# Spreading 1 / sum with full-size constants, and the last 64 keys of v in a zero-padded tile

## The chip, the cores and the metric

The kernel runs on one core of a Trainium2 chip. The metric is the device time of one execution in microseconds (us). One execution of each kernel was also recorded by the hardware profiler; the engines in it are PE (TensorE matmul), PEld (TensorE weight load), DVE (VectorE), ACT (ScalarE), POOL (GpSimd) and SP (SyncE, which issues most DMAs).

## The reference

Four batches, eight heads of size 64, 576 positions. Per head, scores = q k^T / 8; in each row the 32 largest scores are kept, exponentiated, divided by their sum and multiplied by v. The heads, side by side, make x (576 x 512 per batch), which goes through a gated value projection and a phase mixer:

```python
scores = np.where(scores >= kth, scores, -1e9); scores -= scores.max(-1)
attn = np.exp(scores); attn = attn / (attn.sum(-1) + 1e-9); x = attn @ v
x = (sigmoid(causal_conv5(x)) * (x @ w_val)) @ w_out
theta = x @ w_theta; u = x + w_tok_r @ (x * cos(theta)) + w_tok_i @ (x * sin(theta))
out = u + relu(u @ w_ch)
```

## The kernel before

The attention runs over tiles of 128 query rows. A unit u is a pair of heads (j = 0, 1) of one batch; its 576 query rows are handled in two parts, x = 0 (rows 0 to 255) and x = 1 (rows 256 to 575). There are 16 units, so 32 parts. For each tile PE computes the scores from split q and k (L536, L537), ACT moves them out of PSUM (L550), DVE searches the largest ones (L572 to L599, with help of ACT L585 and POOL L593), ACT takes the exponential (L193), DVE masks and sums (L652), and PE transposes the result: four full 128 x 128 transposes (L665) that ACT copies into pT (L684), and one of the last 64 keys (L669), which uses free columns of a scores bank; ACT copies it into slot 8 of pT (L673). In slot 8 the last 64 keys of head j = 0 lie in partitions 0 to 63, those of j = 1 in partitions 64 to 127.

When a part has all its tiles, `close` ends it:

- the product px with v (L758) has ten matmuls: five chunks c of keys times two heads j. Head j's result goes to PSUM partitions 64j to 64j + 63. Chunks 0 to 3 have 128 keys each, chunk 4 has 64, whose v lies in partitions 64j to 64j + 63 of the fifth slot of the tile v2;
- 1 / sum (tile rs, one column for each query tile and head: 4 columns for x = 0, 5 for x = 1) is transposed on PE (L714) and copied by ACT into rT (L717, 4 or 5 partitions by 128 columns);
- `columns(m)`, for m = 0 and 1, spreads a row of rT over the 64 partitions of its head: one matmul for each j at L731, whose stationary operand is a column of the identity matrix, repeated 64 times. For x = 1 and m = 1 there is also a fifth row, the 64 last queries of both heads, spread by a matmul for each j at L734. These matmuls use free columns of a scores bank: m = 0 stands behind L669 in the first bank, m = 1 behind the scores of the second. ACT copies the bank's part into rb (L738);
- DVE multiplies px by rb (L776).

```python
nc.tensor.matmul(spare[r, :P], row(2 * j + m), rT[:n], start=True, stop=True,
                 skip_group_check=True)
```

Each fp32 matmul is two records of PE in the trace; a transpose is one, and so is a matmul of the split (fp32r) operands. DVE and ACT follow the order in which the program is written. PE, POOL and SP are put in order by a scheduler when the program is built, each instruction as soon as it is due. Between the attention steps PE is given pieces of the projections and of the mixer (L507, L805, L1107, L1126). v of a unit is loaded by three DMAs of SP into the one buffer v2 (L223, and L227 twice); they wait until the px before has read it. The constants are made by POOL at the program's start (L162 to L176).

Of the kernel before, what the change touches and what calls it, by code (L numbers as in the profile page):

```python
# [11 lines left out]
F32 = mybir.dt.float32  # L12
# [78 lines left out]
def mixer(ctx, tc, qT, kT, vt, w_val, conv_t, w_out, w_theta, w_tok, w_ch, out, flag):  # L91
    nc = tc.nc
    safe = flag is None
    P = 128
# [4 lines left out]
    NF = S // P  # L99
    REM = S - NF * P  # L100
# [14 lines left out]
    cp = ctx.enter_context(tc.tile_pool(name="cp", bufs=1))  # L115
    io = ctx.enter_context(tc.tile_pool(name="io", bufs=1))
    sp = ctx.enter_context(tc.tile_pool(name="sp", bufs=1))
    wk = ctx.enter_context(tc.tile_pool(name="wk", bufs=1))
# [44 lines left out]
    ident = cp.tile([P, P], F32, name="ident")  # L163
# [8 lines left out]
    nc.gpsimd.memset(trig_bias[64:], 0.0)  # L172
    half_pi = cp.tile([P, 1], F32, name="half_pi")
    nc.gpsimd.memset(half_pi, math.pi / 2)
    magic = cp.tile([P, 1], F32, name="magic")
    nc.gpsimd.memset(magic, MAGIC)  # L176

# [40 lines left out]
    def load_v(part):  # L218
        u = part["u"]
        b, hp = divmod(u, NP)  # L220
        v2 = io.tile([P, NF + 1, P], F32, tag="v2", name=f"v2_{u}_{part['x']}")
        vu = vt[b, :, hp * P : (hp + 1) * P]
        nc.sync.dma_start(v2[:, :NF, :], vu[: NF * P].rearrange("(c p) d -> p c d", p=P))  # L223

        for j in range(2):
            r = slice(REM * j, REM * j + REM)
            nc.sync.dma_start(v2[r, NF, 64 * j : 64 * j + 64], vu[NF * P :, 64 * j : 64 * j + 64])  # L227
        part["v"] = v2
        if u // NP not in SPLIT:
            parts[u, 1]["v"] = v2  # L230
# [457 lines left out]
    def diagonal(hp):  # L688

        if not diagonals:  # L690
            all_of = ml.tile([P, 2 * NC * ROOM[1]], F32, tag="room1", name="diagonals")
            diagonals["all"] = all_of[:, : NP * KW * P].rearrange("p (u k w) -> p u k w", u=NP, k=KW)
        if hp not in diagonals:
            diagonals[hp] = diagonals["all"][:, hp]
            nc.gpsimd.tensor_tensor(diagonals[hp], ident.unsqueeze(1).broadcast_to([P, KW, P]),
                                    W["conv"][:, hp, :].unsqueeze(2).broadcast_to([P, KW, P]), ALU.mult)
        return diagonals[hp]

    def close(part):

        u, x = part["u"], part["x"]
        b, hp = divmod(u, NP)
        lo, hi = COLS[x]
        w = hi - lo
        n = 4 + x
        rs = wk.tile([P, 5], F32, tag="rs", name=f"rs_{u}_{x}", bufs=2)
        rT = wk.tile([5, P], F32, tag="rT", name=f"rT_{u}_{x}")
        rb = wk.tile([P, S - CUT], F32, tag="rb", name=f"rb_{u}_{x}")
        nc.gpsimd.tensor_scalar(rs[:, :n], part["sums"][:, :n], 1e-9, None, ALU.add)
        nc.vector.reciprocal(rs[:, :n], rs[:, :n])  # L710
        done = set()

        def rows(spare):
            nc.tensor.transpose(spare[:n, :P], rs[:, :n], ident)  # L714

            def f():
                nc.scalar.copy(rT[:n], spare[:n, :P])  # L717
                done.add("rows")
            return f

        def row(k):
            return ident[:n, k : k + 1].broadcast_to([n, 64])

        def columns(m):


            def on_pe(spare):
                c = P + REM * (m * x)
                for j in range(2):
                    r = slice(64 * j, 64 * j + 64)  # L730
                    nc.tensor.matmul(spare[r, :P], row(2 * j + m), rT[:n], start=True, stop=True,  # L731
                                     skip_group_check=True)
                    if c > P:
                        nc.tensor.matmul(spare[r, P:c], row(4), rT[:n, r], start=True, stop=True,  # L734
                                         skip_group_check=True)

                def f():
                    nc.scalar.copy(rb[:, m * P : m * P + c], spare[:, :c])  # L738
                    done.add(m)
                return f  # L740
            return on_pe

        extras.append((P, rows))
        yield
        yield
        asked = "rows" in done
        if asked:
            extras.extend((P + REM * (x * m), columns(m)) for m in range(2))
        yield
        if x == 0:  # L750
            drain(("val", (u - 5) // NP))
        v, pT = part["v"], part["pT"]
        owed[0] -= 8.3 * w
        px = ps_m.tile([P, w], F32, tag="m", name=f"px_{u}_{x}")
        for c in range(NF + 1):
            for j in range(2):
                r, k = (slice(0, P), j * NF + c) if c < NF else (slice(REM * j, REM * j + REM), 2 * NF)
                nc.tensor.matmul(px[64 * j : 64 * j + 64, :], v[r, c, 64 * j : 64 * j + 64], pT[r, k, :],  # L758
                                 start=(c == 0), stop=(c == NF), skip_group_check=True)
        if x == 0:  # L760
            xt = sp.tile([P, PAD + S], F32, tag="xT", name=f"xT_{u}", bufs=5)
            nc.gpsimd.memset(xt[:, :PAD], 0.0)
            xT.setdefault(b, []).append(xt)
        xt = xT[b][hp]
        yield
        while "rows" not in done:
            yield
            yield
        if not asked:
            extras.extend((P + REM * (x * m), columns(m)) for m in range(2))  # L770
        yield
        yield
        while 1 not in done:
            yield
            yield
        nc.vector.tensor_tensor(xt[:, PAD + lo : PAD + hi], px, rb[:, :w], ALU.mult)  # L776
        there.add((u, x))
        split = b in SPLIT
        if not split and x == 0:
            return  # L780
        if split and x:
            g = gate[b][hp]
        else:
            drain(("gate", (u - GB) // NP))
            g = sp.tile([P, S], F32, tag="gp", name=f"gp_{u}", bufs=GB)
            gate.setdefault(b, []).append(g)
        if not split:
            lo = 0
        g = g[:, lo:hi]
        cw = W["conv"]  # L790
        if hp == NP - 1:
            jobs.append(front(b, (x,) if split else (0, 1)))
            if x:
                jobs.append(back(b))
        yield
        yield
        while lacking["conv"]:
            yield
            yield
        taps = [xt[:, k + lo : k + hi] for k in range(KW)]  # L800
        if split:
            owed[0] -= 1.675 * KW * (hi - lo)
            ps = ps_m.tile([P, hi - lo], F32, tag="m", name=f"pconv_{u}_{x}")
            for k in range(KW):
                nc.tensor.matmul(ps, diagonal(hp)[:, k, :], taps[k], start=(k == 0), stop=(k == KW - 1))  # L805
            yield
            yield
            tabled(g, ps, AF.Tanh, scale=0.5)
            ready.add((u, x))
            return  # L810
        nc.scalar.activation(g, taps[0], AF.Copy, scale=cw[:, hp, 0:1])
        for k in CT:
            ct = wk.tile([P, S], F32, tag="ct", name=f"ct_{u}_{x}_{k}")[:, : g.shape[1]]
            nc.scalar.activation(ct, taps[k], AF.Copy, scale=cw[:, hp, k : k + 1])
            nc.gpsimd.tensor_tensor(g, g, ct, ALU.add)
            yield
            yield
        if not CT:
            yield
            yield  # L820
        rest = [k for k in range(1, KW) if k not in CT]
        for k in rest:
            nc.vector.scalar_tensor_tensor(g, taps[k], cw[:, hp, k : k + 1], g, ALU.mult, ALU.add)
            if k == rest[1] and len(rest) > 2 or k == rest[-1]:
                yield
                yield
        tabled(g, g, AF.Tanh, scale=0.5)
        ready.add((u, x))
# [355 lines left out]
    for b in range(B):  # L1184
        late = b == B - 1
        f = 1.275 if b in THREE else 1.675
# [19 lines left out]
    def drain(key):  # L1206

        n = 0
        while key[1] >= 0 and key not in done:
            n += 1  # L1210
            assert n < 1000, (key, [(j.gi_frame.f_code.co_name, j.gi_frame.f_lineno, j.gi_frame.f_locals.get('b')) for j in jobs], sorted(map(str, done))[-40:], len(later), len(mid))
            run_mid()
            now, later[:] = list(later), []
            run(now)
            work(DRAIN)
# [24 lines left out]
    for k, part in enumerate(order):  # L1240
        i0 = part["tiles"][0].i
        u, x = part["u"], part["x"]
# [5 lines left out]
        elif split or x == 0:  # L1248
            when = (i0 - 7, i0 - 5, i0 - 5, i0 - 4, i0 - 3) if split or i0 and order[k - 1]["x"] and order[k - 1]["u"] // NP in SPLIT else (i0 - 9, i0 - 8, i0 - 7, i0 - 6, i0 - 3)
            a = (u, x if split else None)  # L1250
            for step, do in zip(when, (load_heads, split_high, split_low, *(
                    lambda u, x, j=j: double(u, j, x) for j in range(2)))):
# [144 lines left out]
```

## Time and profile before

| | us |
|---|---|
| median of 3 runs (lowest, highest) | 849.69 (846.92, 850.99) |
| the profiled execution's own time | 849.38 |
| its span, first to last instruction | 847.3 |
| PE busy | 754.7 (89%) |
| DVE busy | 679.4 (80%) |
| ACT busy | 640.3 (76%) |
| POOL busy | 438.5 (52%) |

The profile is of one execution. Matmuls are pipelined, so the length of a record tells little; how far apart the starts of two records lie tells what PE needs between them. The chain of work that ended last goes back from the last instruction, at each step to what released it or to the instruction before it on its engine: what stands on it set the time.

### The profile page before, as it was taken

How to read it: one execution, taken by the hardware profiler on the slowest of the kernel's cores; microseconds unless marked ns; L12 is line 12 of the kernel's file. 1: busy time of each engine (PE TensorE's matmuls, PEld its weight loads, DVE VectorE, ACT ScalarE, POOL GpSimd, SP SyncE). 2: the span in 40 equal slices, each digit the busy share in tenths (PEclk: the TensorE clock that was granted, in tenths of full speed). 3: DMA queues.
4: the chain of work that ended last, by engine and by line, in shares of the span. 5: the costliest groups of instructions: out<-in, count | busy, mean ns of one | idle time of the engine just before them, and what ended most of it. 6: DMA issues, size and time to landing. Idle time of an engine off the chain costs nothing.

```text
span 847.3 us, 16018 instructions
## 1 busy us (share of the span) xinstructions
PE 754.7 (89%) x4606; PEld 577.5 (68%) x4606; DVE 679.4 (80%) x2786; ACT 640.3 (76%) x1573; POOL 438.5 (52%) x575
## 2 busy tenths in 40 slices
PE   4478999969898899899699989999999899999995
PEld 3345667535655666677587666768897666798895
DVE  6999999879977888899889879989998686353521
ACT  6688898889778777889689887789987784336511
POOL 4876665545544545457667725537796143004600
PEclk9997799979999899999899999999999999999998
DMA  6566665634440243337455543234664300061002
GB/s 171 140 167 189 163 171 161 176 90 127 117 107 15 58 144 82 94 77 240 112 171 168 151 136 83 44 83 100 184 176 122 100 1 15 1 211 45 2 1 61
DMA packets 73602, 94.37 MB, mean 111 GB/s; under 512 B 13728, under 2 KB 37152, under 8 KB 73504
## 3 DMA queue, kind: packets, MB, share of 16 engines
q1 hardware_dynamic: 73184, 92.82, 40.3%
q8 instruction: 39, 0.64, 0.3%
q14 instruction: 59, 0.48, 0.2%
q10 hardware_dynamic: 320, 0.43, 0.2%
HBM read 49.96 MB, written 13.11 MB: 74 GB/s over the span
## 4 chain that ended last, share of the span: by engine, by line
PE 48%; DVE 27%; ACT 11%; POOL 6%; issue 4%; DMA 3%; SPq 1%; ACTq 0%; POOLq 0%
PE py L1107 8%; PE px L758 7%; DVE cand L572 6%; PE pval L507 5%; DVE thrs L599 4%; PE px2t L507 4%; PE pth L507 4%; PE ph L507 3%; PE pt L665 3%; DVE s L652 3%; PE py L1126 3%; PE ps L536 3%; POOL y L593 2%; DVE cand L578 2%; PE ps L537 2%
## 5 line engine op out<-in xcount | busy, mean ns | idle before, releaser
L593 POOL TENSOR_TENSOR y<-s,n 128x576 f32<-128x576 f32 x144 | 190.6, 1324 | 164.8 <-DVE thrs L599 118.6
L572 DVE MAX8 cand<-s 128x8 f32<-128x96 f32 x864 | 210.2, 244 | 1.4 <-ACT s L550 1.4
L652 DVE SCALAR_TENSOR_TENSOR s<-s,thrs,e 128x576 f32<-128x576 f32 x144 | 139.4, 968 | 9.7 <-ACT e L193 9.7
L585 ACT ACTIVATE n<-s,tops 128x576 bf16<-128x576 f32 x144 | 112.0, 778 | 39.6 <-POOL y L593 18.7
L550 ACT ACTIVATE s<-ps 128x256 f32<-128x256 f32 (+1 forms) x288 | 103.7, 406 | 32.9 <-PE ps L731 15.8
L665 PE MATMUL pt<-ident,s 128*128 128x128 f32 x576 | 96.2, 288 | 26.7 <-ACT pT L684 12.6
L1107 PE MATMUL py<-w_tok,z 128*128 128x256 f32 (+1 forms) x432 | 116.8, 410 | 3.4 <-DVE z L966 3.4
L599 DVE MAX8 thrs<-y 128x8 f32<-128x584 f32 x144 | 109.3, 759 | 6.8 <-POOL y L594 6.4
L758 PE MATMUL px<-pT,v 128*64 128x256 f32 (+3 forms) x640 | 106.7, 432 | 9.0 <-ACT pT L684 8.8
L193 ACT ACTIVATE e<-s,least 128x576 f32<-128x576 f32 x144 | 110.7, 769 | 0.5 <-DVE s L652 0.4
L665 PEld LDWEIGHTS pt<-ident,s 128*128 128x128 f32 x576 | 68.8, 145 | 55.6 <-ACT pT L684 22.4
L536 PE MATMUL ps<-kh_None,q 128*128 128x256 f32 x240 | 92.0, 390 | 4.1 <-ACT s L550 2.2
L684 ACT COPY pT<-pt 128x512 f32<-128x512 f32 x128 | 73.1, 571 | 28.5 <-PE pt L665 15.4
L1107 PEld LDWEIGHTS py<-w_tok,z 128*128 128x128 f32 x432 | 77.8, 191 | 24.0 <-DVE z L966 5.0
L758 PEld LDWEIGHTS px<-pT,v 128*64 128x64 f32 (+1 forms) x640 | 43.6, 140 | 57.6 <-issue 26.5
L576 DVE MAX8 tops<-cand 128x8 f32<-128x48 f32 x432 | 82.7, 191 | 0.1
L537 PE MATMUL ps<-kl_None,q 128*128 128x256 f32 x240 | 71.4, 300 | 0.0
L536 PEld LDWEIGHTS ps<-kh_None,q 128*128 128x128 f32 x240 | 46.4, 193 | 21.1 <-ACT s L550 6.1
L536 PE MATMUL ps<-kh,q 128*128 128x256 f32 (+1 forms) x80 | 37.5, 475 | 20.3 <-ACT s L550 8.6
L578 DVE MATCH_REPLACE8 cand<-tops,cand 128x48 f32<-128x48 f32 x288 | 55.1, 191 | 0.0
L673 ACT COPY pT<-ps 64x128 f32<-64x128 f32 (+1 forms) x160 | 39.3, 245 | 12.6 <-PE ps L669 5.8
L537 PEld LDWEIGHTS ps<-kl_None,q 128*128 128x128 f32 x240 | 47.0, 196 | 2.5 <-issue 0.9
(209 smaller groups left out, 1693.4 us busy)
## 6 DMA issues: line engine op xcount, KB each, us to landing
kh_None<-kh_None SPq DMA_DIRECT2D x48, 144.0 KB, 2.6
kl_None<-kl_None SPq DMA_DIRECT2D x48, 144.0 KB, 2.7
v<-in_vt_dram SPq DMA_DIRECT2D x20, 256.0 KB, 3.5
out_dram<-x2T SPq DMA_DIRECT2D x16, 256.0 KB, 3.2
w<-ch SPq DMA_DIRECT2D x16, 256.0 KB, 4.3
w<-theta SPq DMA_DIRECT2D x16, 256.0 KB, 5.4
raw_hi<-in_w_tok_dram SPq DMA_DIRECT2D x14, 256.0 KB, 4.1
kh<-kh SPq DMA_DIRECT2D x24, 144.0 KB, 2.6
```

The source lines that it names most:

```text
L193: ins = nc.scalar.activation(out, src, func, **more).ins
L507: nc.tensor.matmul(ps[o : o + n], x, y, start=(i + k == 0), stop=(i == last and k == len(ways) - 1), skip_group_check=(n < P))
L536: nc.tensor.matmul(bank[:, :w], q2, kh[:, lo:hi], start=(j == js[0]), stop=False)
L537: nc.tensor.matmul(bank[:, :w], q2, kl[:, lo:hi], start=False, stop=(j == js[-1]))
L572: nc.vector.max(d["cand"][:, k, 8 * x : 8 * x + 8], s_tiles[i][:, x * SUB : (x + 1) * SUB])
L585: nc.scalar.activation(n, s_tiles[i], AF.Sign, bias=d["tops"][:, k, KC - 1 : KC], scale=-(1.0 + 2.0 ** -22), accum_out=acc)
L593: nc.gpsimd.tensor_tensor(y[:, :S], s_tiles[i], d.pop(("n", k)), ALU.mult)
L599: nc.vector.max(thrs[:, N - 1 - i : N - 1 - i + NK], d.pop(("y", k)))
L652: nc.vector.scalar_tensor_tensor(p, p, thr(i), e.exp, ALU.is_ge, ALU.mult, accum_out=part["sums"][:, e.slot : e.slot + 1])
L665: nc.tensor.transpose(e.pt[:, c, :], p[:, c * P : (c + 1) * P], ident)
L758: nc.tensor.matmul(px[64 * j : 64 * j + 64, :], v[r, c, 64 * j : 64 * j + 64], pT[r, k, :], start=(c == 0), stop=(c == NF), skip_group_che ...
L1107: nc.tensor.matmul(ps, z[:, m * P : (m + 1) * P], W["tok"][:, w, lo:hi], start=(i + k == 0), stop=(i == NF))
```

## The change

Three constants are added. `spread` (128 x 7 x 64) holds, in the order 0, 2, 1, 3, none, 4, none, the selectors of rows of rT: a slot for row k has ones in partition k and zeros elsewhere, a slot "none" is zero. Two neighbouring slots make a stationary operand of 128 x 128. `rT` becomes one tile of 128 partitions whose rows from 5 on stay zero. `v_last` (128 x 128) takes the last 64 keys of both heads, each head's 64 columns with zeros in the other head's partitions.

At `columns(m)` one matmul takes the place of the two at L731: slots (0, 2) or (1, 3) spread the rows of both heads over all 128 partitions. For the fifth row there are still two matmuls of 64 columns, now with slots (4, none) and (none, 4), which add up in PSUM. At px the fifth chunk multiplies all 128 partitions of slot 8 of pT by v_last.

```diff
+    spread = cp.tile([P, 7, 64], F32, name="spread")
+    nc.gpsimd.memset(spread, 0.0)
+    for i, k in enumerate((0, 2, 1, 3, None, 4)):
+        if k is not None:
+            nc.gpsimd.tensor_copy(spread[:, i, :], ident[:, k : k + 1].broadcast_to([P, 64]))
+    rT = cp.tile([P, P], F32, name="rT")
+    nc.gpsimd.memset(rT, 0.0)
+    v_last = cp.tile([P, P], F32, name="v_last")
+    nc.gpsimd.memset(v_last, 0.0)
...
-        v2 = io.tile([P, NF + 1, P], F32, tag="v2", name=f"v2_{u}_{part['x']}")
+        v2 = io.tile([P, NF, P], F32, tag="v2", name=f"v2_{u}_{part['x']}")
...
-            nc.sync.dma_start(v2[r, NF, 64 * j : 64 * j + 64], vu[NF * P :, 64 * j : 64 * j + 64])
+            nc.sync.dma_start(v_last[r, 64 * j : 64 * j + 64], vu[NF * P :, 64 * j : 64 * j + 64])
...
-        rT = wk.tile([5, P], F32, tag="rT", name=f"rT_{u}_{x}")
...
-        def row(k):
-            return ident[:n, k : k + 1].broadcast_to([n, 64])
+        def rows_of(i):
+            return spread[:, i : i + 2, :].rearrange("p a w -> p (a w)")
...
-                for j in range(2):
-                    r = slice(64 * j, 64 * j + 64)
-                    nc.tensor.matmul(spare[r, :P], row(2 * j + m), rT[:n], start=True, stop=True,
-                                     skip_group_check=True)
-                    if c > P:
-                        nc.tensor.matmul(spare[r, P:c], row(4), rT[:n, r], start=True, stop=True,
-                                         skip_group_check=True)
+                nc.tensor.matmul(spare[:, :P], rows_of(2 * m), rT, start=True, stop=True,
+                                 skip_group_check=True)
+                for j in range(2 if c > P else 0):
+                    nc.tensor.matmul(spare[:, P:c], rows_of(5 - j), rT[:, 64 * j : 64 * j + 64],
+                                     start=(j == 0), stop=(j == 1), skip_group_check=True)
...
-                r, k = (slice(0, P), j * NF + c) if c < NF else (slice(REM * j, REM * j + REM), 2 * NF)
-                nc.tensor.matmul(px[64 * j : 64 * j + 64, :], v[r, c, 64 * j : 64 * j + 64], pT[r, k, :],
+                d = slice(64 * j, 64 * j + 64)
+                of_v, k = (v[:, c, d], j * NF + c) if c < NF else (v_last[:, d], 2 * NF)
+                nc.tensor.matmul(px[d, :], of_v, pT[:, k, :],
                                  start=(c == 0), stop=(c == NF), skip_group_check=True)
```

On PE the first block of a closing part of x = 1 stood so before (ps is a scores bank; a row gives the tiles, and the partitions by columns that are written):

```order
L669 MATMUL ps_0_1869<-ident,s_1270 64x128
L731 MATMUL ps_0_1869<-rT_1_1695,ident 64x128 x2
L536 MATMUL ps_256_1875<-kh_3_1_1737,q_87 128x320
L537 MATMUL ps_256_1875<-kl_3_1_1738,q_87 128x320
L731 MATMUL ps_256_1875<-rT_1_1695,ident 64x128
L734 MATMUL ps_256_1875<-rT_1_1695,ident 64x64
L665 MATMUL pt_1917<-ident,s_1325 128x128 x4
```

and stands so now:

```order
L678 MATMUL ps_0_1867<-ident,s_1274 64x128
L737 MATMUL ps_0_1867<-rT,spread 128x128
L545 MATMUL ps_256_1872<-kh_3_1_1735,q_87 128x320
L546 MATMUL ps_256_1872<-kl_3_1_1736,q_87 128x320
L737 MATMUL ps_256_1872<-rT,spread 128x128
L740 MATMUL ps_256_1872<-rT,spread 128x64 x2
L674 MATMUL pt_1913<-ident,s_1327 128x128 x4
```

The place is the same; two matmuls of 64 partitions became one of 128 (before, the pair L731, L734 stood twice in the second bank, once for each j).

On SP the load of v for unit 3 of batch 0 stood so before:

```order
L227 DMA v_2_0_1214<-in_vt_dram 64x64
L216 DMA kl_1_1218<-in_kT_dram 128x576
L216 DMA ql_1_1220<-in_qT_dram 128x320
L309 DMA raw_hi_120<-in_w_theta_dram 128x512
L309 DMA raw_hi_121<-in_w_theta_dram 128x512
L309 DMA raw_lo_122<-in_w_theta_dram 128x512
L223 DMA v_3_0_1463<-in_vt_dram 128x4x128
```

and stands so now:

```order
L236 DMA v_last<-in_vt_dram 64x64
L225 DMA kl_1_1222<-in_kT_dram 128x576
L232 DMA v_3_0_1464<-in_vt_dram 128x4x128
L225 DMA ql_1_1224<-in_qT_dram 128x320
L318 DMA raw_hi_131<-in_w_theta_dram 128x512
L318 DMA raw_hi_132<-in_w_theta_dram 128x512
L318 DMA raw_lo_133<-in_w_theta_dram 128x512
```

The load of the first four chunks moved ahead of the load of q and of three loads of weights.

On POOL, at the start, the new constants stand between the making of the identity and the last small ones:

```order
L174 MEMSET half_pi 128x1
L176 MEMSET spread 128x448
masks.py:199 AFFINE_SELECT ident<-ident 128x128
L181 MEMSET rT 128x128
L179 COPY spread<-ident 128x64 x5
L183 MEMSET v_last 128x128
L185 MEMSET magic 128x1
```

Before, none of the rows on spread, rT and v_last was there, and the identity was made last.

## Rows read from the trace of the kernel before

**Rows 1.** Stretches: us, busy us (instructions) of PE, PEld, DVE, ACT, POOL; clock, DMA.

```profile
0.00:510.00 510.00, 433.41 (x2457) 311.14 (x2458) 452.19 (x1957) 424.22 (x1068) 294.82 (x411) 0.95 0.50 134
510.00:650.00 140.00, 138.15 (x948) 110.24 (x948) 131.25 (x569) 118.21 (x298) 93.79 (x116) 1.00 0.45 120
650.00:740.00 90.00, 86.33 (x522) 63.92 (x521) 54.40 (x187) 58.09 (x131) 24.35 (x32) 1.00 0.09 28
```

**Rows 2.** The same view of L758 (px) alone, PE and PEld.

```profile
0.00:510.00 510.00, 71.48 (x400) 28.36 (x400) 0.95 0.50 134
510.00:740.00 230.00, 35.24 (x240) 15.23 (x240) 1.00 0.31 84
```

**Rows 3.** Chain that ended last, shares by line: of 0:510, then of 510:740.

```profile
by line: DVE cand L572 7.8%; issue 6.1%; DVE thrs L599 5.9%; PE px L758 5.8%; DVE s L652 4.1%; PE pval L507 3.9%; POOL y L593 3.4%; PE ps L536 3.1%; ACT n L585 3.1%; PE pconv L805 3.0%; DVE cand L578 3.0%; ACT e L193 2.8%; PE pth L507 2.8%;
...
by line: PE py L1107 23.8%; PE px L758 13.5%; PE pt L665 7.4%; PE pth L507 4.8%; PE ph L507 4.1%; PE ps L536 3.8%; PE px2t L507 3.7%; DVE cand L572 3.5%; PE ps L731 3.4%; PE ps L537 3.1%; DVE s L652 2.9%; DVE gp L823 2.7%; DVE thrs L599 2.7
```

**Rows 4.** Timeline of PE, full-size work alone: start us, length, instruction.

```profile
527.49 0.27 PE L669 MATMUL ps<-ident,s 128*64 128x128 f32 x1
...
527.75 0.32 PE L537 MATMUL ps<-kl_None,q 128*128 128x320 f32 x1
527.90 0.60 PE L665 MATMUL pt<-ident,s 128*128 128x128 f32 x4
528.34 0.38 PE L1107 MATMUL py<-w_tok,z 128*128 128x256 f32 x1
```

**Rows 5.** Timeline of PE around the blocks of a part x = 1.

```profile
138.46 0.27 PE L669 MATMUL ps<-ident,s 128*64 128x128 f32 x1
138.67 0.43 PE L731 MATMUL ps<-rT,ident 5*64 5x128 f32 x4
...
139.28 0.30 PE L537 MATMUL ps<-kl,q 128*128 128x320 f32 x1
...
140.00 0.66 PE L665 MATMUL pt<-ident,s 128*128 128x128 f32 x4
140.49 0.81 PE L507 MATMUL px2t<-gp,w_out 128*128 128x256 f32 x3
```

**Rows 6.** Timeline of PE around the second block of a part x = 0.

```profile
341.88 0.30 PE L537 MATMUL ps<-kl_None,q 128*128 128x320 f32 x1
...
342.48 0.55 PE L665 MATMUL pt<-ident,s 128*128 128x128 f32 x3
```

**Rows 7.** Timeline of PE at the end of a px, looked at moment by moment.

```profile
244.11 0.60 PE L758 MATMUL px<-pT,v 128*64 128x256 f32 x4
...
244.32 0.60 PE L758 MATMUL px<-pT,v 128*64 128x256 f32 x4
...
244.85 0.43 PE L758 MATMUL px<-pT,v 64*64 64x256 f32 x2
...
245.12 0.38 PE L758 MATMUL px<-pT,v 64*64 64x256 f32 x2
```

**Rows 8.** Timeline of PE where both blocks of a part stand together.

```profile
692.08 0.27 PE L669 MATMUL ps<-ident,s 128*64 128x128 f32 x1
...
692.86 0.28 PE L714 MATMUL ps<-ident,rs 128*5 128x128 f32 x1
```

**Rows 9.** Timeline of PEld, in the stretch of rows 4.

```profile
527.75 0.51 PEld L665 LDWEIGHTS pt<-ident,s 128*128 128x128 f32 x4
```

**Rows 10.** Timeline of POOL at the start; in brackets its idle time before.

```profile
1.95 0.30 POOL masks.py:199 TENSOR_SCALAR_AFFINE_SELECT ident<-ident 128x128 f32<-128x128 f32 x1
12.44 0.73 POOL L291 TENSOR_TENSOR q<-raw,q 64x256 fp32r<-64x256 f32 x1 [10.18 <-ACT q L289]
```

**Rows 11.** Timeline of SP's DMA issues around the moved load of v.

```profile
92.76 0.36 SPq L216 DMA_DIRECT2D ql<-in_qT_dram  x1
...
94.87 0.38 SPq L223 DMA_DIRECT2D v<-in_vt_dram  x1
```

**Rows 12.** SP's own waits: total us, times, longest.

```profile
SPq L223 <- PE px L758: 85.3, 13, 31.6
```

More of the change, by code (lines that the diff above doesn't have):

```diff
@@ L220, in load_v @@
         b, hp = divmod(u, NP)
-        v2 = io.tile([P, NF + 1, P], F32, tag="v2", name=f"v2_{u}_{part['x']}")
+        v2 = io.tile([P, NF, P], F32, tag="v2", name=f"v2_{u}_{part['x']}")
         vu = vt[b, :, hp * P : (hp + 1) * P]
-        nc.sync.dma_start(v2[:, :NF, :], vu[: NF * P].rearrange("(c p) d -> p c d", p=P))
+        nc.sync.dma_start(v2, vu[: NF * P].rearrange("(c p) d -> p c d", p=P))
         for j in range(2):
             r = slice(REM * j, REM * j + REM)
-            nc.sync.dma_start(v2[r, NF, 64 * j : 64 * j + 64], vu[NF * P :, 64 * j : 64 * j + 64])
+            nc.sync.dma_start(v_last[r, 64 * j : 64 * j + 64], vu[NF * P :, 64 * j : 64 * j + 64])
         part["v"] = v2
```

## The prediction

> **What bounds the kernel now.** I read the stretches first, then the chain of work that ended last in two of them, then the timeline of PE around the work that changes. PE is busy 433 of the first 510 us, DVE 452 and ACT 424: no engine is the bound for long [rows 1]. From 510 to 650 us PE is busy 138.2 of 140, DVE 131.3; from 650 to 740 PE 86.3 of 90 and DVE only 54.4. After 740 us nothing changes, since px is all in the first 740 us [rows 2]. The chain agrees: before 510 us its largest line is DVE's search, after it PE's L1107 and px [rows 3].
>
> How much of PE's work in a closing part lies on the chain can be read from px. In 0 to 510 us px has 5.8% of the chain, 29.6 us, and is busy 71.5 us [rows 2, 3]: 41%. In 510 to 740 us it has 13.5%, 31.1 us, of 35.2 busy: 88%.
>
> The timeline shows what small matmuls cost. Where PE does full-size work alone, the scores after a transpose L669 follow at once: from L669 to the second L537 it takes 0.26 us, from that L537 to the transposes L665 0.15, and the four transposes 0.44, so 0.11 each [rows 4]. With a spreading block between them the first way takes 0.82 us [rows 5], so a pair at L731 costs 0.56 us. The pair is four records of 128 columns; they start two by two, and the two of one pass nearly together, which is seen from their common length of 0.43. Work of two passes should need 0.22 us (0.11 each, as the transposes). The other 0.34 is spent on going into the small shape and out again: 0.20 us from L669 to L731 instead of 0.11, and so on.
>
> **The change, part by part.** All PE prices are for the granted clock of 1.00, 2.4 GHz; it is 0.95 on average in the first 510 us [rows 1], and what is gained there at the lower level is left out.
>
> *First block (m = 0), 32 times.* A pair becomes one full-width matmul of two records. No row shows such a record with 128 columns; the nearest are a transpose, 0.11 us, and a px record of 256 columns, 0.21 us from start to start, 244.11 to 244.32 [rows 7]. I take 0.11, since the columns are half as many. The block then costs 0.22 instead of 0.56: 0.34 us less. At 0.21 it would be 0.14 less.
>
> *Second block (m = 1).* For x = 0 L537 to L665 takes 0.60 us [rows 6] instead of 0.15; the first transpose behind the small shape takes about 0.05 longer, as 0.49 for the four against 0.44 shows [rows 4, 5]. That is 0.50; the new one costs 0.22: 0.28 less. For x = 1 the two matmuls of the fifth row are in it. From L537 to what follows the transposes it takes 1.21 us [rows 5] against 0.59 [rows 4], so 0.62. Now there are two records of 128 columns and four of 64, which no longer go two by two. [...] The new block is 6 x 0.11 = 0.65, 0.03 dearer than before (0.19 cheaper at the lower end).
>
> *Last chunk of px, 32 times.* The records of 128 rows follow each other every 0.21 us. Into the chunk of 64 rows it takes 0.53 us for two such steps (244.32 to 244.85; the records of 244.54 lie between), and the step inside takes 0.27 [rows 7]. With v_last the chunk is of the same shape as the others: 0.10 + 0.05 = 0.15 us less.
>
> So PE gains 0.34 + 0.28 + 0.15 = 0.77 us at a part x = 0 and 0.34 - 0.03 + 0.15 = 0.46 at x = 1. In 0 to 510 us there are 20 parts (400 records of px, 20 each [rows 2]), ten of each kind: 12.3 us. In 510 to 740 us there are twelve: 7.4 us. In four of these, two of each kind, both blocks stand together, and PE goes into the small shape once instead of twice. There 0.78 us pass from L669 to what follows the eight records [rows 8], so the blocks cost 0.67; four full-width records cost 0.44, and the gain is 0.23 instead of 0.62. Taking this 0.39 off four times leaves 5.8 us. PE alone gains 18.1 us.
>
> On the chain this is 12.3 x 0.41 = 5.0 and 5.8 x 0.88 = 5.1 us. The chain is one path, though, and others are just behind it. Before 510 us DVE and ACT are as busy as PE [rows 1], so I count half of the 5.0; after 510 us PE is the bound, and I count all. **That is 7.6 us.**
>
> *What I cost at nothing.* POOL makes spread, rT and v_last at the start: five copies of 64 columns and three memsets. The nearest row is 0.30 us for 128 columns [rows 10]; nine times that (the memset of 448 columns counted as two) is 2.7 us, and POOL waits 10.2 us there for ACT. If that cover were gone, it would be 2.7 us at most. The loads of v_last carry the same bytes by the same queue as before, and both old and new tiles are single buffers. px of head 0 now waits for head 1's last rows as well; at most it exchanges a wait with the matmul right behind it. ACT, DVE and the number of DMAs are unchanged. The load of v of unit 3 moves ahead of one load of q and three of weights; in the trace v was issued 2.1 us after q [rows 11], so 2.1 us is the most it holds them up, and I take none of it, since it is let go a chunk earlier than before.
>
> The sum is made against the profiled execution, 849.4 us, 0.3 below the median of 849.7: 849.4 - 7.6 = **841.8 us**.
>
> **Rivals.** *PE is not what ends last.* Where DVE is busy over 90% of the time, a faster PE only waits for it. Then the gain is left where DVE has room, 650 to 740 us [rows 1]: four px (0.6), the blocks that stand together (2 x 0.23, the two of x = 1 counted as nothing) and one part's first and second block (0.31), 1.4 us: 848.0. For it speaks that DVE has 9 us of idle time in 510 to 650 us; against it that these 9 us are more than the gain there, and px's 88%.
>
> *A full-width record costs 0.21 us, or its weights aren't loaded under the record before.* Then the first block gains 0.14, the second of x = 0 0.08, that of x = 1 loses some 0.45 (two records of 0.21 and four of 0.16, 1.06 against 0.62). A part gains 0.37 or loses 0.16, and on the chain as above (0.41 of ten of each, half of it counted, and 0.88 of six of each) the gain is some 1.5 us: 847.9. Against it, four loads of 128 rows run in 0.51 us while matmuls on the same rows start every 0.11 [rows 4, 9]. The Trainium skill (TensorE: Matmul & The Clock Gate, section The mechanism) has the rule that a weight load overlaps running matmuls only where the row group differs; by it this rival would be the forecast, and the trace of this kernel does not agree with it. The same page (section Part 3: Packing small matmuls — row/col tiling) says that small matmuls gain by running side by side in the array, which speaks against undoing a pair; here the rows show that the pairs do run together, and that going in and out costs more than they save, but for the fifth row.
>
> *Slower: SP's queue.* SP issues in order. If the moved load of v must wait for px, q and three weight loads wait behind it, and scores and conversions behind those. SP's 13 waits of this kind take 85.3 us, 6.6 on average, up to 31.6 [rows 12]. With an average wait there, and only the 1.4 us of the first rival gained, it is 849.4 + 6.6 - 1.4 = 854.6. It decides from a delay of some 6 us on. Against it, the place in the trace bounds it at 2.1 us [rows 11].
>
> **The numbers.** A measurement of this kernel can tell 0.5%, 4.2 us, from no change. The forecast gets 0.69, the first rival 0.20, the second 0.05, the slower one 0.06. The forecast's own range goes from 839.3 (all of the 10.1 us on the chain) to about 845 (only what comes after 510 us, 844.3), and further down to where part of the other 8 us of PE's gain counts too, 835, since a freed bank also lets ACT start sooner. The range of 835 to 848.2 takes the first two rivals in and leaves out the slower one and the tails. Faster by over 0.5%: 0.67, within it 0.26 (the first two rivals and a piece of the forecast), slower 0.07.
>
> **What would show it.** In the new profile L678 (the old L669) to the second L546 should take 0.48 us over a spreading block, the two records of L737 lying 0.11 apart, and the four of L740 0.44. px should show a step of 0.21 to its end, with no form of 64 rows. PE's busy time should fall by some 15 us or more, and PEld's idle time before the small loads go. The chain should still be mostly PE from 510 to 740 us. I am wrong if the records of L737 or L740 lie 0.2 us apart, if DVE's busy share in 510 to 650 us rises to the full with the same end, or if SP stands at the load of v around 93 us.

## The result, and the profile after

The changed kernel takes 838.56 us (median of 4 runs, 837.97 to 839.01) against 849.61 us: a ratio of 0.9873, with a 95% interval of 0.9848 to 0.9898. The time forecast was 841.8 us, with a range of 835.0 to 848.2. The profiled execution took 838.7 us, 10.7 less than that of before. From its page (parts 1 and 4):

```profile
span 836.9 us, 15761 instructions
...
PE 734.5 (88%) x4478; PEld 584.1 (70%) x4478; DVE 677.7 (81%) x2786; ACT 639.4 (76%) x1573; POOL 440.5 (53%) x583
...
PE 39%; DVE 32%; ACT 13%; POOL 6%; issue 5%; DMA 4%; SPq 0%; ACTq 0%; POOLq 0%
PE py L1114 8%; DVE cand L581 7%; DVE thrs L608 5%; PE px L765 5%; DVE s L661 4%; PE pth L516 4%; PE ph L516 3%; PE px2t L516 3%; PE pval L516 3%; PE py L1133 3%; DVE cand L587 3%; DVE tops L585 3%; PE pt L674 3%; ACT n L594 2%; POOL y L602 2%
```

PE is busy for 20.2 us less; the busy time of DVE, ACT and POOL moved by 2 us or less, and that of PEld rose by 6.6 (from 577.5). (L536, L537, L665, L669, L714, L731, L734 and L758 are now L545, L546, L674, L678, L722, L737, L740 and L765.)

The timeline of PE around the blocks of a part x = 1, the place of [rows 5]:

```profile
137.40 0.27 PE L678 MATMUL ps<-ident,s 128*64 128x128 f32 x1
137.51 0.39 PE L737 MATMUL ps<-rT,spread 128*128 128x128 f32 x2
137.65 0.39 PE L545 MATMUL ps<-kh,q 128*128 128x320 f32 x1
137.88 0.31 PE L546 MATMUL ps<-kl,q 128*128 128x320 f32 x1
138.03 0.38 PE L737 MATMUL ps<-rT,spread 128*128 128x128 f32 x2
138.25 0.56 PE L740 MATMUL ps<-rT,spread 128*128 128x64 f32 x4
138.64 0.61 PE L674 MATMUL pt<-ident,s 128*128 128x128 f32 x4
139.08 0.81 PE L516 MATMUL px2t<-gp,w_out 128*128 128x256 f32 x3
```

From L678 to the second L546 it now takes 0.48 us instead of 0.82, L737 follows L678 after 0.11, and L545 follows at once. The second block, from L546 to L516, takes 1.20 us, where it took 1.21. Around the second block of a part x = 0, from L546 to L674, it takes 0.36 us instead of 0.60 [rows 6]:

```profile
337.45 0.31 PE L546 MATMUL ps<-kl_None,q 128*128 128x320 f32 x1
337.59 0.38 PE L737 MATMUL ps<-rT,spread 128*128 128x128 f32 x2
337.81 0.49 PE L674 MATMUL pt<-ident,s 128*128 128x128 f32 x3
```

At the end of the px of [rows 7], looked at moment by moment, two steps into the last chunk take 0.43 us (242.74 to 243.17) instead of 0.53 and the step inside it 0.21 instead of 0.27:

```profile
242.74 0.60 PE L765 MATMUL px<-pT,v 128*64 128x256 f32 x4
...
243.17 0.39 PE L765 MATMUL px<-pT,v_last 128*64 128x256 f32 x2
...
243.38 0.39 PE L765 MATMUL px<-pT,v_last 128*64 128x256 f32 x2
...
243.70 0.44 PE L674 MATMUL pt<-ident,s 128*128 128x128 f32 x2
```

Where both blocks of a part x = 0 stand together, from L678 to L722, it takes 0.56 us instead of 0.78 [rows 8]:

```profile
682.43 0.27 PE L678 MATMUL ps<-ident,s 128*64 128x128 f32 x1
682.54 0.61 PE L737 MATMUL ps<-rT,spread 128*128 128x128 f32 x4
682.99 0.27 PE L722 MATMUL ps<-ident,rs 128*5 128x128 f32 x1
683.10 0.60 PE L674 MATMUL pt<-ident,s 128*128 128x128 f32 x4
```

The weight loads show the way in, too. Before, PEld stood idle ahead of a block's first load, which began together with its matmul (138.67 us); now the load begins with L678's matmul (137.40), 0.11 us ahead of its own:

```profile
138.66 0.19 PEld L731 LDWEIGHTS ps<-rT,ident 5*64 5x64 f32 x4 [0.20 <-issue]
...
137.40 0.30 PEld L737 LDWEIGHTS ps<-rT,spread 128*128 128x128 f32 x2
```

Where the time came from is seen when the start of a part's px (its first record in the timeline) is laid beside that of before:

| start of px, us | 5th part | 9th | 13th | 17th | 21st | 25th | 29th | 32nd | span |
|---|---|---|---|---|---|---|---|---|---|
| before | 131.2 | 243.0 | 334.7 | 402.0 | 510.4 | 590.3 | 685.6 | 730.4 | 847.3 |
| after | 129.6 | 241.4 | 331.2 | 397.3 | 505.1 | 582.4 | 676.1 | 719.9 | 836.9 |
| less | 1.6 | 1.6 | 3.5 | 4.7 | 5.3 | 7.9 | 9.5 | 10.5 | 10.4 |

5.3 us are gained until the 21st part, where the prediction drew its line of 510 us, 5.2 us from there to the last px, and nothing behind it. The stretches, with the columns of [rows 1]:

```profile
0.00:510.00 510.00, 425.07 (x2409) 317.04 (x2410) 458.67 (x1982) 429.54 (x1084) 300.09 (x424) 0.96 0.50 134
510.00:650.00 140.00, 136.94 (x943) 117.17 (x942) 128.03 (x563) 119.61 (x302) 94.20 (x113) 1.00 0.44 118
650.00:740.00 90.00, 86.32 (x525) 68.10 (x525) 55.40 (x178) 55.00 (x124) 21.95 (x28) 1.00 0.12 39
```

DVE has not filled up in 510 to 650 us: 128.0 of 140, a little less than before.

### The profile page after: what moved, and what is told of

Its sections match the earlier page's. It is cut to its first block, busy times and chain, and to the rows that moved or that the text cites. A ratio compares the mean times of both kernels' runs of the same rounds, so it can differ in the third digit from the quotient of the medians.

```text
span 836.9 us, 15761 instructions
## 1 busy us (share of the span) xinstructions
PE 734.5 (88%) x4478; PEld 584.1 (70%) x4478; DVE 677.7 (81%) x2786; ACT 639.4 (76%) x1573; POOL 440.5 (53%) x583
## 4 chain that ended last, share of the span: by engine, by line
PE 39%; DVE 32%; ACT 13%; POOL 6%; issue 5%; DMA 4%; SPq 0%; ACTq 0%; POOLq 0%
PE py L1114 8%; DVE cand L581 7%; DVE thrs L608 5%; PE px L765 5%; DVE s L661 4%; PE pth L516 4%; PE ph L516 3%; PE px2t L516 3%; PE pval L516 3%; PE py L1133 3%; DVE cand L587 3%; DVE tops L585 3%; PE pt L674 3%; ACT n L594 2%; POOL y L602 2%
## 5 line engine op out<-in xcount | busy, mean ns | idle before, releaser
L661 DVE SCALAR_TENSOR_TENSOR s<-s,thrs,e 128x576 f32<-128x576 f32 x144 | 137.7, 956 | 9.7 <-ACT e L202 9.7
L1114 PE MATMUL py<-w_tok,z 128*128 128x256 f32 (+1 forms) x432 | 118.8, 416 | 1.7 <-DVE z L973 1.7
L674 PE MATMUL pt<-ident,s 128*128 128x128 f32 x576 | 95.3, 286 | 28.4 <-ACT pT L693 15.4
L674 PEld LDWEIGHTS pt<-ident,s 128*128 128x128 f32 x576 | 69.0, 145 | 56.5 <-ACT pT L693 25.9
L545 PE MATMUL ps<-kh_None,q 128*128 128x256 f32 x240 | 92.0, 390 | 5.2 <-ACT rb L744 2.5
L1114 PEld LDWEIGHTS py<-w_tok,z 128*128 128x128 f32 x432 | 79.6, 195 | 22.3 <-DVE z L973 2.5
L765 PE MATMUL px<-pT,v 128*64 128x256 f32 (+1 forms) x512 | 84.5, 431 | 10.1 <-ACT pT L693 10.1
L546 PE MATMUL ps<-kl_None,q 128*128 128x256 f32 x240 | 71.5, 301 | 0.0
L765 PEld LDWEIGHTS px<-pT,v 128*64 128x64 f32 x512 | 37.1, 141 | 43.4 <-issue 12.5
L545 PEld LDWEIGHTS ps<-kh_None,q 128*128 128x128 f32 x240 | 46.7, 195 | 20.2 <-ACT s L559 8.3
L545 PE MATMUL ps<-kh,q 128*128 128x256 f32 (+1 forms) x80 | 35.7, 454 | 24.3 <-ACT s L559 11.0
L546 PEld LDWEIGHTS ps<-kl_None,q 128*128 128x128 f32 x240 | 47.1, 196 | 2.3 <-issue 0.9
```

What stands on the lines that cost most here:

```text
L545: nc.tensor.matmul(bank[:, :w], q2, kh[:, lo:hi], start=(j == js[0]), stop=False)
L546: nc.tensor.matmul(bank[:, :w], q2, kl[:, lo:hi], start=False, stop=(j == js[-1]))
L661: nc.vector.scalar_tensor_tensor(p, p, thr(i), e.exp, ALU.is_ge, ALU.mult, accum_out=part["sums"][:, e.slot : e.slot + 1])
L674: nc.tensor.transpose(e.pt[:, c, :], p[:, c * P : (c + 1) * P], ident)
L765: nc.tensor.matmul(px[d, :], of_v, pT[:, k, :], start=(c == 0), stop=(c == NF), skip_group_check=True)
L1114: nc.tensor.matmul(ps, z[:, m * P : (m + 1) * P], W["tok"][:, w, lo:hi], start=(i + k == 0), stop=(i == NF))
```

## The experiments

The theory was that PE loses time each time it goes from full-size work into another shape and out again, and that this time is on the chain before and after 510 us in the shares of px. Its rivals were that the gain came from v's loads and buffer, that few rows alone or halves of the columns alone cost, and that part of the gain is only passed on or is taken back by DVE. Each kernel was compared with the kernel before on the same chip.

**One part of the change each.** The first run undoes v_last, the second undoes the spreading:

```diff
+        v2 = io.tile([P, NF + 1, P], F32, tag="v2", name=f"v2_{u}_{part['x']}")
...
+                r, k = (slice(0, P), j * NF + c) if c < NF else (slice(REM * j, REM * j + REM), 2 * NF)
+                nc.tensor.matmul(px[64 * j : 64 * j + 64, :], v[r, c, 64 * j : 64 * j + 64], pT[r, k, :],
```

> Only 1 / sum is spread by full-size constants; v is loaded and multiplied as before. If the gain is PE no longer going into small shapes and out again, PE keeps 13.3 of the 18.1 us it gains (the other 4.8 are 32 last chunks at 0.15), and the time keeps the same share of its 11.0 us: 8.1 us less than before, about 841.5. If the gain came from v (a buffer that is let go earlier, loads that stand earlier in SP's queue), the time is that of before, 849.6.

Measured: 841.29 us against 848.39, a ratio of 0.9913 (0.9892 to 0.9934).

```diff
+                    nc.tensor.matmul(spare[r, :P], row(2 * j + m), rT[:n], start=True, stop=True,
+                                     skip_group_check=True)
...
```

> Only the last 64 keys of v have a tile with zeros; 1 / sum is spread as before. By the small-shape theory PE gains 4.8 us and the time 2.9: about 846.7, with the step into the last chunk of px at 0.21 us instead of 0.31. If v's loads are what mattered, 840 or less.

Measured: 845.42 us against 848.39, a ratio of 0.9967 (0.9954 to 0.9979). Both came out near what the theory said: 7.1 us less, where 8.1 was expected, and 3.0, where 2.9 was. The two together make 10.1 of the whole change's 11.0. The rival that v's loads matter fails in the first run, which keeps the old loads and most of the gain.

**Which side of the shape costs.** The constants stay; the first run uses only the 4 or 5 rows that hold something, the second goes in pairs of 64 columns over all 128 rows:

```diff
-            return spread[:, i : i + 2, :].rearrange("p a w -> p (a w)")
+            return spread[:n, i : i + 2, :].rearrange("p a w -> p (a w)")
...
-                nc.tensor.matmul(spare[:, :P], rows_of(2 * m), rT, start=True, stop=True,
+                nc.tensor.matmul(spare[:, :P], rows_of(2 * m), rT[:n], start=True, stop=True,
...
```

> The spreading matmuls have all 128 columns but only the 4 or 5 rows that are used, so that the shape differs from full size in its rows alone. If any other shape costs the way in and out, the first block costs about 0.56 us as before and the time is about that of v alone, 846.7. If only halves of the columns cost, L678 to the second L546 stays at 0.48 us and the time at 838.6.

```diff
-                nc.tensor.matmul(spare[:, :P], rows_of(2 * m), rT, start=True, stop=True,
-                                 skip_group_check=True)
+                for j in range(2):
+                    r = slice(64 * j, 64 * j + 64)
+                    nc.tensor.matmul(spare[r, :P], spread[:, 2 * m + j, :], rT, start=True, stop=True,
+                                     skip_group_check=True)
...
```

> The spreading matmuls have all 128 rows, but go in pairs of 64 columns as before, so that the shape differs from full size in its columns alone. If any other shape costs the way in and out, the block costs about 0.56 us and the time is about 846.7. If only few rows cost, the pair runs side by side at 0.22 us, the four small records of the fifth row too, and the time is 838.6 or a little less.

Measured: 847.14 us with few rows (ratio 0.9986, 0.9975 to 0.9996) and 844.17 with half the columns (0.9951, 0.9935 to 0.9968), against 848.39. The times lie near that of v_last alone, so that neither keeps the gain of the spreading; with half the columns it is 1.3 us better than v_last alone and 2.5 under its forecast, but the two intervals overlap. The timelines are clearer than the times. With few rows:

```profile
138.74 0.27 PE L678 MATMUL ps<-ident,s 128*64 128x128 f32 x1
138.94 0.48 PE L737 MATMUL ps<-rT,spread 5*128 5x128 f32 x2
139.35 0.42 PE L545 MATMUL ps<-kh,q 128*128 128x320 f32 x1
139.60 0.31 PE L546 MATMUL ps<-kl,q 128*128 128x320 f32 x1
```

and with half the columns (L739 is the spreading line there):

```profile
137.39 0.27 PE L678 MATMUL ps<-ident,s 128*64 128x128 f32 x1
137.59 0.44 PE L739 MATMUL ps<-rT,spread 128*64 128x128 f32 x4
137.96 0.42 PE L545 MATMUL ps<-kh,q 128*128 128x320 f32 x1
138.21 0.31 PE L546 MATMUL ps<-kl,q 128*128 128x320 f32 x1
```

From L678 to the second L546 it takes 0.86 and 0.82 us, not 0.48. The way in is 0.20 us in both, as before the change. So it is neither the number of rows nor that of columns, but that the shape is not the one of the work around. With few rows the second record starts 0.21 us behind the first. Where four records of L737 stand together in that run, looked at moment by moment, only the first step is that long and the next is 0.11:

```profile
690.07 0.71 PE L737 MATMUL ps<-rT,spread 4*128 4x128 f32 x4
690.28 0.38 PE L737 MATMUL ps<-rT,spread 4*128 4x128 f32 x2
690.39 0.38 PE L737 MATMUL ps<-rT,spread 4*128 4x128 f32 x2
```

So the longer step belongs to the way in, and not to a record that runs without a partner.

**Which parts gain.** `FROM` is 10, so that the 20 parts of units 0 to 9 keep the small shapes; the second run has the condition turned round:

```diff
+                if u < FROM:
+                    for j in range(2):
+                        r = slice(64 * j, 64 * j + 64)
+                        nc.tensor.matmul(spare[r, :P], row(2 * j + m), rT[:n], start=True, stop=True,
+                                         skip_group_check=True)
...
+                r = slice(64 * j, 64 * j + 64) if c == NF and u < FROM else slice(0, P)
```

> The small shapes are kept in the first 20 parts (spreading and last chunk of px), and the change is made in the last 12 alone. The forecast's count is 5.1 us for these, so about 844.5; the landmarks of the two traces (part by part 5.5 us until 510 us, 4.9 behind) say about 844.7. If the later parts only pass on what the earlier ones gain, 849.

> The other way round: the change in the first 20 parts alone. The forecast counted 2.5 us there, half of the chain's 5.0: 847.1. By the landmarks it is 5.5 us: about 844.1. If what is gained early is caught up by DVE later, 849.

Measured: the last 12 parts alone 844.13 us against 848.31 (ratio 0.9943, 0.9921 to 0.9964), the first 20 alone 843.57 (0.9945, 0.9928 to 0.9961). They are worth 4.2 and 4.7 us, or 4.8 and 4.7 by the ratios. The start of px shows it again: with the last 12 alone the 21st px starts at 510.6 us, as before, and the last at 725.5, 4.9 earlier; with the first 20 alone the 21st is 7.4 us earlier (this execution was the fastest of its runs) and the last 7.5. What is gained early is kept, and the last parts gain without the first.

**More work of PE.** The changed kernel with each spreading matmul of 128 columns made three times, which leaves its result as it is:

```diff
+                for _ in range(3):
+                    nc.tensor.matmul(spare[:, :P], rows_of(2 * m), rT, start=True, stop=True,
+                                     skip_group_check=True)
```

> The changed kernel with each spreading matmul of 128 columns made three times over: 64 blocks get two full-size matmuls more, 0.22 us each, 28.2 us of PE in all, with nothing else. If PE's time is what counts, by px's share of the chain as it was before (0.41 of the first 40 blocks, 0.88 of the last 24) the time rises by 16.5 us over the changed kernel, to 855; by the share in the changed kernel's own trace (0.27 and 0.80) by 13, to 852. If the gain was a matter of waits and not of PE's time, it rises by less than 4.

Measured: 853.09 us against 848.31, a ratio of 1.0060 (1.0043 to 1.0077), 14.5 us over the changed kernel's 838.56, or 15.9 by the two ratios. A block in its timeline (L738 is the spreading line):

```profile
336.90 0.27 PE L678 MATMUL ps<-ident,s 128*64 128x128 f32 x1
337.01 0.83 PE L738 MATMUL ps<-rT,spread 128*128 128x128 f32 x6
337.60 0.39 PE L545 MATMUL ps<-kh_None,q 128*128 128x320 f32 x1
337.83 0.31 PE L546 MATMUL ps<-kl_None,q 128*128 128x320 f32 x1
```

From L678 to L546 it takes 0.93 us, 0.45 more than with one, so 64 blocks add 28.5 us to PE, and half of them arrive in the time. That lies between the two counts, 13 and 16.5, and speaks against a gain of waits alone, which was to give less than 4. In the profiled execution, the fastest of the four, the 21st px starts at 507.5 us, only 2.4 behind the changed kernel's, though the 40 blocks before it have 17.8 us more of PE; the last px starts 11.4 behind, so that the other 24 blocks, with 10.7 us more, cost 9.0. The late share is as counted, 0.8. The early one, 0.13, is below both 0.41 and 0.27; the granted clock was higher than in the changed kernel (1.00 against 0.97 in the first 100 us), and how much that covers was not separated.

**A version that goes on from there.** In the order of the program px still breaks into pieces, and each piece is a way into another shape and out. PE begins px with head 0, whose probabilities are ready before those of head 1, and fills the wait with full-size work. Turning the heads round makes it begin later and in fewer pieces:

```diff
-            for j in range(2):
+            for j in (1, 0):
                 d = slice(64 * j, 64 * j + 64)
```

> The changed kernel with the heads of px in the other order, so that px begins with head 1, whose probabilities are ready last, and PE leaves full-size work for px less often: 52 stretches in another shape instead of 65 in the order of the program. At some 0.35 us for each way in and out PE gains 4.6 us; most lie before 510 us, where 0.4 counts: 1.8 us, 836.8. If starting px early was worth more than the ways in and out, the time is that of the changed kernel or more, 838.6 and up.

> The changed kernel once more, beside the run of the other order on the same chip: 838.6, a ratio of 0.987 to the kernel before.

> The run with head 1 first once more, on the same chip: 834.4.

Measured: 834.35 us (ratio 0.9844, 0.9830 to 0.9857), beside the changed kernel's 838.56 on the same chip (0.9876, 0.9859 to 0.9893), and 836.53 (0.9862, 0.9846 to 0.9878) the second time. It is faster than the changed kernel by 4.2 us in the first comparison, with intervals just apart; in the second, which had no run of the changed kernel beside it, by some 1.2 going by the ratios. The forecasts, 836.8 and 834.4, were missed by 2.5 us one way and 2.1 the other. PE is busy for 726.3 and 724.9 us in the two profiles, against 734.3 of the changed kernel in its second one, which is more than the 4.6 us that were counted; why is open.

One step further, px begins with the chunk that is ready last of all:

```diff
-        for c in range(NF + 1):
+        for c in (NF, *range(NF)):
...
```

> As the run with head 1 first, and px begins with the chunk of the last 64 keys, which is ready last of all: all but two px stand in one piece in the order of the program (41 stretches in another shape, not 52). PE gains another 11 x 0.35 = 3.9 us; by the share of 0.4 that is 1.5: 832.8. If px now begins so late that DVE waits for it, 835 or more.

Measured: 839.51 us against 848.72, a ratio of 0.9892 (0.9876 to 0.9907), slower than with head 1 first, on the same chip. This step missed its forecast by 6.7 us. Waits of PE's weight loads for ACT's copy into pT, with head 1 first:

```profile
PEld pt L674 <- ACT pT L693: 22.8, 19, 6.6
...
PEld px L765 <- ACT pT L693: 15.9, 9, 8.1
```

and with the last chunk first:

```profile
PEld pt L674 <- ACT pT L693: 38.2, 26, 8.1
...
PEld px L765 <- ACT pT L693: 0.2, 1, 0.2
```

The wait has moved from px to the transposes; the sum of the two lines is 38.4 us, where it was 38.7. PE stands idle for 109.2 us of its span (838.5 less 729.3 busy), against 106.2 and 108.0 in the two runs with head 1 first. Its busy time is 3.0 and 4.4 us longer than in these, half and four fifths of the difference in span, although it leaves full-size work less often. So much of the loss is work that took longer: the mean granted clock was 0.956 to 0.960 in the five executions, against 0.963 to 0.968 in the nine with head 1 first, and in the profiles 0.93 from 300 to 510 us, against 0.96. Why the clock was lower was not tried.

## Why the prediction was right, and what it mis-sized

*The prices on PE.* The first block was to cost 0.22 us instead of 0.56: it does (0.82 to 0.48). The second of x = 0 was to gain 0.28: 0.24 from L546 to L674, and the first transpose's 0.05. That of x = 1 was to be 0.03 dearer and is 0.01 cheaper. No row of before has a record of 64 columns behind 128 columns of weights, for which the sum takes 0.11; the four records of L740 take 0.39 us, not 0.44, since the second starts 0.06 behind the first and the others 0.11 apart. The last chunk gains 0.15 as said (0.10 and 0.05), the blocks that stand together for x = 0 0.22 (0.23 was said).

In all 18.1 us were to go from PE, and its busy time fell by 20.2. The nearness of the two proves less than it seems to, since the granted clock, the third figure from the end, is also higher in the first 200 us. Before:

```profile
0.00:100.00 100.00, 65.32 (x285) 43.42 (x285) 90.25 (x408) 76.47 (x200) 64.27 (x111) 0.92 0.65 171
100.00:200.00 100.00, 87.68 (x458) 60.42 (x455) 90.08 (x402) 88.67 (x235) 56.09 (x79) 0.89 0.54 139
```

and after:

```profile
0.00:100.00 100.00, 61.38 (x277) 42.38 (x277) 90.01 (x408) 76.33 (x200) 65.93 (x119) 0.97 0.63 170
100.00:200.00 100.00, 84.01 (x450) 59.16 (x451) 91.90 (x408) 90.35 (x240) 56.76 (x81) 0.95 0.55 141
```

PE's busy time fell by 7.6 us there. What the clock can do by itself is seen from the run with half the columns, whose blocks cost what those of v_last alone do: with 0.97 and 0.95 in these stretches, against 0.92 and 0.89, PE is busy for 6.3 us less in them than with v_last alone, and the whole time is 1.3 us better. So some of the gain before 510 us may be the clock's; no run separates the two. The prices of the blocks stand without it: those of [rows 8] lie where the clock is 1.00 before and after.

*The share that counts.* "I count half of the 5.0" is the step that was off. Until the 21st part 5.3 us were gained, not 2.5: about what px's share of the chain gives in full. The run with the first 20 parts alone gains 4.7 us (3.3 to 6.1 by its interval), and half is outside. That DVE and ACT are as busy as PE there was taken for paths close behind the chain; they were far enough behind for this much. Before, the chain had these shares by engine:

```profile
PE 48%; DVE 27%; ACT 11%; POOL 6%; issue 4%; DMA 3%; SPq 1%; ACTq 0%; POOLq 0%
```

Now PE has 39% and DVE 32%, and in the changed kernel's second profile 33% and 35%, so that the chain has moved towards DVE. After 510 us, where the granted clock is 1.00 before and after, 5.1 us were counted and 5.2 gained. The fit before 510 us should not be read too closely: a part of the early gain may be the clock's, and in the run with more work of PE the early share came out at 0.13.

*What was costed at nothing.* POOL's constants fit in its idle time: from 1.66 to 3.57 us, 1.9 us in which the identity's own step of 0.31 stands too, against the bound of 2.7, with 8.84 us left idle:

```profile
1.66 0.48 POOL L176 MEMSET spread<- 128x448 f32 x1
...
3.57 0.11 POOL L185 MEMSET magic<- 128x1 f32 x1
...
12.69 0.73 POOL L300 TENSOR_TENSOR q<-raw,q 64x256 fp32r<-64x256 f32 x1 [8.84 <-ACT q L298]
```

The moved load of v does stand in front of q's, within the bound of 2.1 us:

```profile
92.88 0.53 SPq L225 DMA_DIRECT2D kl<-in_kT_dram  x1
94.10 0.39 SPq L232 DMA_DIRECT2D v<-in_vt_dram  x1
94.58 0.45 SPq L225 DMA_DIRECT2D ql<-in_qT_dram  x1
```

q is issued 1.70 us behind kl, where it was 0.64 (92.12 to 92.76 us before). The starts of px in the 5th to 8th parts, 1.6, 1.1, 1.2 and 3.2 us earlier than before, show no loss from it.

*The rivals.* DVE did not fill up, and 5.3 us came from where the first rival gave nothing. The records of L737 lie 0.11 us apart, so that 0.21 does not hold. The Trainium skill (TensorE: Matmul & The Clock Gate, section The mechanism) says that weight loads overlap running matmuls only where the row group differs; this trace does not agree with that sentence, since L737's first load, of 128 rows, begins at 137.40 us, with L678's matmul, and L737 follows that one after 0.11. The same section also lets a load go ahead into a background weight buffer, which the trace does not contradict. What agrees is the Trainium skill's TensorEngine Tiling (Array Packing), section Key Properties: changing the tiling mode drains the engine. In the trace the first load of a small block waits 0.20 us and the ways in and out are 0.34 us of a block's 0.56, so a pair has to save more than that, and it does so nowhere but in the fifth row.

## What to carry to other kernels

A few small matmuls between full-size ones cost PE more by going in and out of their shape than by their work; padding them with zeros to the shape of their neighbours can be cheaper than using less of the array, and it is the neighbours' shape that counts, not the padding itself. To see it, read the distance of the starts across the block and compare it with the same place without the block. For the time, the share of that work that the chain has in the stretch was a better guide to this gain than half of it. That is one change: work added at the same places cost less than the share in the early parts, and the two changes of the order of px did not come out at it. Look at the granted clock of each stretch before a fall of busy time is put down to the change.

## What the runs showed of the hardware that was not expected

A transpose pays nothing for its shape: L722, with 5 columns of weights, stands between full-size records at 0.11 us (682.99 to 683.10), and L678, with 64 columns, too. In these traces only matmuls that aren't transposes show the 0.20 us on the way in.

Few rows cost no less than half the columns: 0.20 us on the way in with either, and from the start of L737 or L739 to the second L546 0.66 and 0.62.

In the run with more work of PE the mean granted clock of the profiled execution was 0.981, against 0.969 and 0.967 of the changed kernel's two profiles, and PE was busy for only 17.5 us more (752.0), though 28.5 were added. Of the two levels, 1.2 and 2.4 GHz, the higher was granted more of the time there. It was 0.973 to 0.974 in that run's other three executions and 0.961 to 0.974 in the changed kernel's eight; the kernel before, with PE as busy (754.7), had 0.958 to 0.967. So PE's busy time alone does not settle it, and what does was not tried.
